# Float64 weights to float32 pairs by another chain of instructions, on ACT and DVE instead of ACT, DVE and POOL

## The chip, the core and the metric

One core of one Trainium2 chip runs the whole program. The metric is the device time of one execution in microseconds; the kernel before takes 956.41 us (median of three runs, 956.0 to 957.4). A core has five engines that run side by side, each with an in-order queue of its own: PE (matrix products, with its weight loads shown as PEld), DVE (vector), ACT (scalar), POOL (GpSimd) and SP, which here only issues DMAs. Waits between engines go by semaphores.

## The reference

```python
scores = scale * np.matmul(q, k.transpose(0, 1, 3, 2))     # 8 batches, 8 heads, 576 positions, 64 wide
mask_plain = (rel >= 0) & (rel < window)                   # window 32, heads 0 to 3
mask_dil = (rel >= 0) & (rel < window * dilation) & (rel % dilation == 0)   # dilation 4, heads 4 to 7
attn = softmax(np.where(masks, scores, -1e9))
x = np.matmul(attn, v) -> (4608, 512)
h = x @ w_in                                               # 512 to 2048
g = h * np.clip(h + 3.0, 0.0, 6.0) / 6.0
return g @ w_out                                           # 2048 to 512
```

`w_in` and `w_out` come as float64, q, k and v as float32. The kernel gets the float64 words as they are and must make float32 numbers of them on the chip.

## The kernel before, in words

**Feed-forward part.** The 4608 tokens are cut into 12 chunks of 384 (`CH`), the 2048 hidden features into 16 groups of 128 (`NF`, index f). One step is one chunk with one f: `gemm1` (lines 406 to 427) makes h of that group with 12 products of 384 columns (lines 416 to 418), then ACT adds 3 and clips at 0 (line 421, tile t), DVE clips at 6 and multiplies by h (line 422), ACT rounds to the matrix format (line 425, gh) and DVE takes the remainder (line 426, gl). `gemm2` (lines 429 to 443) adds the group's part of the output with 9 products of 512 columns (lines 437 to 439), two steps later (`LAG`). Numbers are kept as a rounded high part and a remainder, so each product is three: high by high, low by high, high by low. `gemm1` has two PSUM tiles, so the products of step n wait for line 422 of step n-2. The first two chunks run interleaved over f (lines 456 to 461), the others one after the other; there are 192 steps.

**Attention part.** The work is cut into 48 trios. The first 12 (`NFIRST`) run ahead of and into the first steps (lines 513 to 523), the rest beside the products of later steps (lines 470 to 480). A trio has scores and values on PE, turns of the tiles (line 245 on PE for the first 12), the softmax on DVE (lines 186 to 191) and ACT (line 193), the division on DVE (lines 200 to 203), and `st_split` (lines 279 to 305): ACT rounds x to xh (line 302), POOL takes the remainder xl (line 305).

**Weights.** Each f has two pieces of 128 x 512 float64 numbers, 32 pieces in all, 512 KB each. SP loads a piece into a staging tile `st` of four rows of 512 words (line 326); rows 0 and 1 hold the words as loaded, rows 2 and 3 are for work. The result goes to `wt[f]`: row 2j the rounded high part (`hi`), row 2j+1 the remainder (`lo`). Staging tiles and `wt` tiles share one pool of 18 buffers, and `wt` tiles stay, so with rising f fewer are left for staging. A conversion goes in three stages, and `convert_beat` (lines 379 to 392) advances up to three pieces by one stage each: split of one piece, join of the next, fields of the one after.

- `cv_fields` (lines 337 to 348): DVE cuts the exponent out of the high word (line 341) and the mantissa bits (line 344), ACT shifts and rebiases the exponent (line 348).
- `cv_join` (lines 350 to 359): DVE adds the low word, scaled, to the mantissa (line 352) and the sign to the exponent (line 355), POOL multiplies both (line 359).
- `cv_split` (lines 361 to 365): ACT rounds (line 363, `hi`), POOL takes the remainder (line 364, `lo`).

**Order.** Within an engine the order is set at build time from priorities: `turn_of` gives each part of a step its place, the beats come once a step and a second time in every other step until step 30 (`BEATS`, `EXTRA`), six of them ahead of the first step (`CB`). `pace` ties the first instructions of a piece, in that ordering, behind the last product that was written down before them; it adds no wait on the chip.

Of the kernel before, what the change touches and what calls it, by code (L numbers as in the profile page):

```python
# [8 lines left out]
F32 = mybir.dt.float32  # L9
F32R = mybir.dt.float32r  # L10
BF16 = mybir.dt.bfloat16
I32 = mybir.dt.int32
U32 = mybir.dt.uint32
I64 = mybir.dt.int64
AF = mybir.ActivationFunctionType
ALU = mybir.AluOpType
AX = mybir.AxisListType

P = 128
# [29 lines left out]
def windowed_attention_ffn(ctx: ExitStack, tc: tile.TileContext, qk, vp, w, mask, out):  # L49
# [23 lines left out]
    nc = tc.nc  # L73
# [20 lines left out]
    const = ctx.enter_context(tc.tile_pool(name="const", bufs=1))  # L94
# [14 lines left out]
    ident_b = mi[:, :P]  # L109
    mask_sb = mi[:, P:].rearrange("p (t x) -> p t x", t=6)  # L110
    ident = const.tile([P, P], F32, name="ident")
    rebias = const.tile([P, 1], F32, name="rebias")
    three = const.tile([P, 1], F32, name="three")


# [4 lines left out]
    for _ in range(WARM):  # L120
        nc.tensor.matmul(idle, lhsT=zeros[:, :P], rhs=zeros[:, P : P + 512], start=True, stop=True)

    nc.gpsimd.memset(rebias, -float(916 << 23))
    nc.gpsimd.memset(three, 3.0)


# [182 lines left out]
    def pace(ins):  # L309

        if "pe" in last:
            tc.add_manual_dep(
                ins.ins, last["pe"].ins.name,
                mybir.DependencyInfo(mybir.DependencyClass.NoSync, mybir.DependencyReason.DATA), reason="pace",
            )
# [5 lines left out]
    wt, staged = {}, {}  # L321
# [8 lines left out]

    def parts(p):
        st = staged[p]
        words = st[:, 0:2].rearrange("p a n -> p (a n)").bitcast(U32).rearrange("p (n w) -> p n w", w=2)
        f, j = divmod(p, 2)
        return words[:, :, 0], words[:, :, 1], st[:, 2], st[:, 3], wt[f][:, 2 * j], wt[f][:, 2 * j + 1]

    def cv_fields(p):
        if p % 2 == 0:
            wt[p // 2] = wpool.tile([P, 4, WN], F32R, name="wt", tag="w")
        _, hi_w, ex, mn, _, _ = parts(p)  # L340
        pace(nc.vector.tensor_scalar(  # L341
            out=ex.bitcast(U32), in0=hi_w, scalar1=0x7FF00000, scalar2=None, op0=ALU.bitwise_and
        ))
        pace(nc.vector.tensor_scalar(  # L344
            out=mn.bitcast(U32), in0=hi_w, scalar1=0xFFFFF, scalar2=0x100000,
            op0=ALU.bitwise_and, op1=ALU.bitwise_or,
        ))
        nc.scalar.activation(ex.bitcast(I32), ex.bitcast(I32), AF.Relu, bias=rebias, scale=8.0)

    def cv_join(p):  # L350
        lo_w, hi_w, ex, mn, _, _ = parts(p)
        nc.vector.scalar_tensor_tensor(  # L352
            out=mn, in0=lo_w, scalar=2.0**-32, in1=mn.bitcast(U32), op0=ALU.mult, op1=ALU.add
        )
        nc.vector.scalar_tensor_tensor(  # L355
            out=ex.bitcast(U32), in0=hi_w, scalar=0x80000000, in1=ex.bitcast(U32),
            op0=ALU.bitwise_and, op1=ALU.bitwise_or,
        )
        nc.gpsimd.tensor_tensor(out=mn, in0=mn, in1=ex, op=ALU.mult)  # L359

    def cv_split(p):
        _, _, _, mn, hi, lo = parts(p)
        nc.scalar.copy(hi, mn)  # L363
        nc.gpsimd.tensor_tensor(out=lo, in0=mn, in1=hi.bitcast(F32), op=ALU.subtract)  # L364
        del staged[p]


# [11 lines left out]
    def convert_beat():  # L379
        if beat["split"] < beat["join"]:  # L380
            cv_split(beat["split"])
            beat["split"] += 1
        if beat["join"] < beat["fields"]:
            cv_join(beat["join"])
            beat["join"] += 1
        p = beat["fields"]
        if p < NP:
            load_ahead(p + 1)
            if p < beat["loaded"]:
                cv_fields(p)  # L390
                beat["fields"] += 1
        load_ahead(p + (AHEAD if "g" in last else AHEAD0))
# [119 lines left out]
    n = 0  # L512
# [106 lines left out]
```

## Time and profile before

| | before |
|---|---|
| median of three runs | 956.41 us |
| the profiled execution's own time | 957.13 us |
| its span, first to last instruction | 955.3 us |
| mean granted TensorE clock | 0.983 |
| busy PE, DVE, ACT, POOL | 905.7, 486.4, 334.0, 151.7 us |
| POOL lines 359 and 364, 32 each | 44.9 and 48.4 us |
| POOL line 305, 72 in all | 59.3 us |

The page of the profile gives busy time by engine, the span in 40 slices with a digit for the busy tenths in each, and the groups of instructions by line with their count, busy time, mean time of one, and the idle time of the engine just before them. The table by windows gives the busy time of each engine in chosen stretches. Busy time of PE counts modelled ends of pipelined products, so a busy PE is not a PE at its full rate.

### The profile page before, as it was taken

The page shows a single profiled execution, that of the slowest core. Times are in us where ns is not written, and L with a number is a line of the kernel's source. Part 1 is how long each engine was busy: PE and PEld are TensorE (multiplying, and loading weights), DVE is VectorE, ACT ScalarE, POOL GpSimd, SP SyncE. Part 2 cuts the span into 40 slices and gives each one's busy share as a digit, 9 for nine tenths or more (in the row PEclk, how much of TensorE's full clock was granted, in tenths as well). Part 3 has the DMA queues.
Part 4 walks back from the last instruction along what each step waited for, and adds up shares of the span by engine and source line. Part 5 has one row for each costly group of instructions (what it writes and reads, how often), then busy time and mean ns, then how long its engine had stood idle before and what let it go on. Part 6 is the DMA issues. An engine that isn't in the chain of part 4 may idle for free.

```text
span 955.3 us, 20665 instructions
## 1 busy us (share of the span) xinstructions
PE 905.7 (95%) x8732; PEld 803.3 (84%) x8732; DVE 486.4 (51%) x934; ACT 334.0 (35%) x629; POOL 151.7 (16%) x142
## 2 busy tenths in 40 slices
PE   7687878999988999999999999999999999999998
PEld 4476767898777898899899898999989888899997
DVE  4879999823445544544543543453444444432221
ACT  3655444433223333332333333322333333322322
POOL 0667566600011000000001001000001001000000
PEclk9889999999989999999999999999999999999999
DMA  9756222102233311311311311311311310100000
GB/s 318 240 197 237 66 70 86 45 11 99 67 85 88 112 50 46 112 49 47 112 50 47 113 48 47 112 49 49 112 48 49 112 30 15 43 5 1 34 1 33
DMA packets 37676, 74.87 MB, mean 78 GB/s; under 512 B 7248, under 2 KB 16464, under 8 KB 37584
## 3 DMA queue, kind: packets, MB, share of 16 engines
q1 hardware_dynamic: 32400, 64.12, 21.4%
q10 hardware_dynamic: 5184, 9.44, 2.7%
q8 instruction: 68, 1.11, 0.5%
q14 instruction: 24, 0.20, 0.1%
HBM read 57.02 MB, written 9.44 MB: 70 GB/s over the span
## 4 chain that ended last, share of the span: by engine, by line
PE 82%; DVE 13%; issue 2%; DMA 2%; ACT 1%; SPq 0%; DVEq 0%
PE ps_o L437 13%; PE ps_h L416 13%; PE ps_h L417 13%; PE ps_h L418 13%; PE ps_o L438 12%; PE ps_o L439 12%; DVE st L344 3%; PE ps_a L174 3%; PE ps_a L156 2%; DVE st L341 2%; DVE st L355 2%; DVE st L352 2%; DVE t L422 1%; DVE gl L426 1%; DMA st<-in_w 1%
## 5 line engine op out<-in xcount | busy, mean ns | idle before, releaser
L416 PE MATMUL ps_h<-xh,wt 128*128 128x384 f32 x768 | 263.2, 343 | 21.6 <-DVE t L422 21.6
L417 PE MATMUL ps_h<-xl,wt 128*128 128x384 f32 x768 | 262.3, 342 | 0.0
L418 PE MATMUL ps_h<-xh,wt 128*128 128x384 f32 x768 | 262.1, 341 | 0.0
L422 DVE SCALAR_TENSOR_TENSOR t<-t,ps_h 128x384 f32<-128x384 f32 x192 | 105.9, 552 | 298.3 <-ACT t L421 277.8
L437 PE MATMUL ps_o<-wt,gh 128*128 128x512 f32 x576 | 229.9, 399 | 0.0
L438 PE MATMUL ps_o<-wt,gh 128*128 128x512 f32 x576 | 226.9, 394 | 0.0
L439 PE MATMUL ps_o<-wt,gl 128*128 128x512 f32 x576 | 222.1, 392 | 4.4 <-DVE gl L426 4.4
L421 ACT ACTIVATE t<-ps_h,three 128x384 f32<-128x384 f32 x192 | 111.2, 579 | 240.0 <-PE ps_h L418 237.8
L416 PEld LDWEIGHTS ps_h<-xh,wt 128*128 128x128 f32 x768 | 145.4, 189 | 34.3 <-DVE t L422 27.2
L426 DVE TENSOR_TENSOR gl<-t,gh 128x384 fp32r<-128x384 f32 x192 | 113.7, 592 | 100.4 <-ACT gh L425 100.4
L305 POOL TENSOR_TENSOR xl<-xf,xh 128x384 fp32r<-128x384 f32 (+3 forms) x72 | 59.3, 836 | 637.2 <-ACT xh L302 636.6
L425 ACT CAST gh<-t 128x384 fp32r<-128x384 f32 x192 | 98.5, 513 | 155.9 <-DVE t L422 152.9
L417 PEld LDWEIGHTS ps_h<-xl,wt 128*128 128x128 f32 x768 | 145.5, 189 | 7.1
L418 PEld LDWEIGHTS ps_h<-xh,wt 128*128 128x128 f32 x768 | 145.8, 190 | 0.2 <-POOL wt L364 0.2
L439 PEld LDWEIGHTS ps_o<-wt,gl 128*128 128x128 f32 x576 | 108.6, 189 | 28.5 <-DVE gl L426 5.7
L437 PEld LDWEIGHTS ps_o<-wt,gh 128*128 128x128 f32 x576 | 109.8, 191 | 18.3
L438 PEld LDWEIGHTS ps_o<-wt,gh 128*128 128x128 f32 x576 | 109.5, 190 | 15.9
L193 ACT ACTIVATE e<-e 128x384 f32<-128x384 f32 x48 | 25.1, 524 | 101.9 <-DVE e L189 101.9
L156 PE MATMUL ps_a<-kq 64*32 64x64 f32 x2304 | 54.7, 225 | 3.5 <-issue 3.3
L359 POOL TENSOR_TENSOR st<-st 128x512 f32<-128x512 f32 x32 | 44.9, 1405 | 43.2 <-DVE st L355 37.1
L156 PEld LDWEIGHTS ps_a<-kq 64*32 64x32 f32 x2304 | 44.5, 107 | 7.4 <-issue 6.6
L364 POOL TENSOR_TENSOR wt<-st,wt 128x512 fp32r<-128x512 f32 x32 | 48.4, 1522 | 12.3 <-ACT wt L363 12.3
(43 smaller groups left out, 544.6 us busy)
## 6 DMA issues: line engine op xcount, KB each, us to landing
kq<-in_qk SPq DMA_DIRECT2D x48, 416.0 KB, 4.6
v<-in_v SPq DMA_DIRECT2D x48, 390.0 KB, 3.6
st<-in_w SPq DMA_DIRECT2D x32, 512.0 KB, 4.6
out<-o ACTq DMA_DIRECT2D x36, 256.0 KB, 2.1
a<-a_t SPq DMA_DIRECT2D x144, 24.0 KB, 1.8
xf<-xf_t SPq DMA_DIRECT2D x144, 24.0 KB, 1.8
mi<-in_mask SPq DMA_DIRECT2D x1, 608.0 KB, 5.0
```

The lines of the kernel that those rows point to most:

```text
L156: last["pe"] = nc.tensor.matmul(ps[at : at + QB, 2 * QB * i : 2 * QB * (i + 1)], lhsT=x[rows, KW + QB * n : KW + QB * (n + 1)], rhs=x[rows ...
L305: eng.tensor_tensor(out=view(xl), in0=src, in1=view(xh).bitcast(F32), op=ALU.subtract)
L416: nc.tensor.matmul(ph, lhsT=wt[f][:, 0, ks], rhs=a, start=(kt == 0), stop=False)
L417: nc.tensor.matmul(ph, lhsT=wt[f][:, 0, ks], rhs=b, start=False, stop=False)
L418: last["pe"] = nc.tensor.matmul(ph, lhsT=wt[f][:, 1, ks], rhs=a, start=False, stop=(kt == NK - 1))
L421: nc.scalar.activation(t, ph, AF.Relu, bias=three, scale=1.0)
L422: nc.vector.scalar_tensor_tensor(out=t, in0=t, scalar=6.0, in1=ph, op0=ALU.min, op1=ALU.mult)
L425: nc.scalar.copy(gh, t)
L426: nc.vector.tensor_tensor(out=gl, in0=t, in1=gh.bitcast(F32), op=ALU.subtract)
L437: nc.tensor.matmul(po[c][tt], lhsT=gh[:, ts], rhs=wt[f][:, 2], start=(f == 0), stop=False)
L438: nc.tensor.matmul(po[c][tt], lhsT=gh[:, ts], rhs=wt[f][:, 3], start=False, stop=False)
L439: last["pe"] = nc.tensor.matmul(po[c][tt], lhsT=gl[:, ts], rhs=wt[f][:, 2], start=False, stop=(f == NF - 1))
```

## The change

The float64 number's high word, read as a float32, is multiplied by a power of two on ACT, which puts the exponent into place for a shift by three bits; the top three bits of the low word come as a rounded integer from a second ACT instruction. DVE shifts, puts the sign in, adds the integer, and takes the remainder after ACT has rounded. The two POOL instructions per piece and the constant `rebias` are gone. The loads, the beats, the tiles and everything outside these functions stay as they are.

```diff
-    rebias = const.tile([P, 1], F32, name="rebias")
...
-    nc.gpsimd.memset(rebias, -float(916 << 23))
...
     def parts(p):
         st = staged[p]
-        words = st[:, 0:2].rearrange("p a n -> p (a n)").bitcast(U32).rearrange("p (n w) -> p n w", w=2)
         f, j = divmod(p, 2)
-        return words[:, :, 0], words[:, :, 1], st[:, 2], st[:, 3], wt[f][:, 2 * j], wt[f][:, 2 * j + 1]
+        words = st[:, 0:2].rearrange("p a n -> p (a n)").rearrange("p (n w) -> p n w", w=2)
+        return words[:, :, 1], words[:, :, 0], st[:, 2], st[:, 3], wt[f][:, 2 * j], wt[f][:, 2 * j + 1]
 
     def cv_fields(p):
         if p % 2 == 0:
             wt[p // 2] = wpool.tile([P, 4, WN], F32R, name="wt", tag="w")
-        _, hi_w, ex, mn, _, _ = parts(p)
-        pace(nc.vector.tensor_scalar(
-            out=ex.bitcast(U32), in0=hi_w, scalar1=0x7FF00000, scalar2=None, op0=ALU.bitwise_and
-        ))
-        pace(nc.vector.tensor_scalar(
-            out=mn.bitcast(U32), in0=hi_w, scalar1=0xFFFFF, scalar2=0x100000,
-            op0=ALU.bitwise_and, op1=ALU.bitwise_or,
-        ))
-        nc.scalar.activation(ex.bitcast(I32), ex.bitcast(I32), AF.Relu, bias=rebias, scale=8.0)
+        hi_w, lo_w, v, a, _, _ = parts(p)
+        pace(nc.scalar.mul(v, hi_w, 2.0**-112))
+        pace(nc.scalar.mul(a.bitcast(U32), lo_w.bitcast(U32), 2.0**-29))
+        nc.vector.tensor_scalar(
+            out=v.bitcast(U32), in0=v.bitcast(U32), scalar1=3, scalar2=None, op0=ALU.logical_shift_left
+        )
 
     def cv_join(p):
-        lo_w, hi_w, ex, mn, _, _ = parts(p)
+        hi_w, _, v, a, hi, _ = parts(p)
         nc.vector.scalar_tensor_tensor(
-            out=mn, in0=lo_w, scalar=2.0**-32, in1=mn.bitcast(U32), op0=ALU.mult, op1=ALU.add
-        )
-        nc.vector.scalar_tensor_tensor(
-            out=ex.bitcast(U32), in0=hi_w, scalar=0x80000000, in1=ex.bitcast(U32),
+            out=v.bitcast(U32), in0=hi_w.bitcast(U32), scalar=0x80000000, in1=v.bitcast(U32),
             op0=ALU.bitwise_and, op1=ALU.bitwise_or,
         )
-        nc.gpsimd.tensor_tensor(out=mn, in0=mn, in1=ex, op=ALU.mult)
+        nc.vector.tensor_tensor(out=v.bitcast(U32), in0=v.bitcast(U32), in1=a.bitcast(U32), op=ALU.add)
+        nc.scalar.copy(hi, v)
 
     def cv_split(p):
-        _, _, _, mn, hi, lo = parts(p)
-        nc.scalar.copy(hi, mn)
-        nc.gpsimd.tensor_tensor(out=lo, in0=mn, in1=hi.bitcast(F32), op=ALU.subtract)
+        _, _, v, _, hi, lo = parts(p)
+        nc.vector.tensor_tensor(out=lo, in0=v, in1=hi.bitcast(F32), op=ALU.subtract)
         del staged[p]
```

## The prediction

> **What bounds the kernel now.** I read the page's slices first, then the table by windows, the groups of instructions in the stage they pointed to, the single lines with their shortest and longest times, and last the waits and the chain. The page's slices are 23.9 us each:
>
> ```profile
> span 955.3 us, 20665 instructions
> ...
> PE   7687878999988999999999999999999999999998
> PEld 4476767898777898899899898999989888899997
> DVE  4879999823445544544543543453444444432221
> ACT  3655444433223333332333333322333333322322
> POOL 0667566600011000000001001000001001000000
> ```
>
> From the ninth slice on PE is full and everything else is loosely used. In slices 3 to 7 it is DVE that stands at nine tenths, and POOL is busy in slices 2 to 8 and hardly after: this is where the weights are converted. The table by windows (busy time and count of PE, PEld, DVE, ACT, POOL, then granted clock, DMA share, GB/s) gives the stage from the end of the first step's products to the end of the conversion, and the one behind it:
>
> ```profile
> 24.00:56.50 32.50, 23.04 (x623) 18.18 (x612) 26.09 (x51) 17.30 (x34) 18.58 (x18) 0.89 0.75 246
> 56.50:191.90 135.40, 113.89 (x661) 98.55 (x662) 126.96 (x166) 65.42 (x121) 87.65 (x63) 0.95 0.31 107
> 192.00:240.00 48.00, 48.00 (x376) 43.40 (x375) 17.17 (x35) 16.09 (x30) 0.00 (x0) 1.00 0.18 62
> ```
>
> In the 135.4 us of the middle row DVE is busy for 126.96; it idles 8.4 us. Behind it PE is busy for 48.00 of 48.00. Line 422 comes once a step, so its starts give the period of a step when PE alone sets it (timeline of DVE, start and duration):
>
> ```profile
> 196.06 0.56 DVE L422 SCALAR_TENSOR_TENSOR t<-t,ps_h 128x384 f32<-128x384 f32 x1 [2.47 <-ACT t L421]
> ...
> 212.70 0.55 DVE L422 SCALAR_TENSOR_TENSOR t<-t,ps_h 128x384 f32<-128x384 f32 x1 [2.47 <-ACT t L421]
> ```
>
> Four periods lie between (starts at 196.06 and 212.70): 4.16 us a step of 21 products. Now the groups of the middle stage alone (count, busy us and mean ns):
>
> ```profile
> L364 POOL TENSOR_TENSOR wt<-st,wt 128x512 fp32r<-128x512 f32 x28 | 42.9, 1542 | 12.3 <-ACT wt L363 12.3
> L359 POOL TENSOR_TENSOR st<-st 128x512 f32<-128x512 f32 x27 | 38.2, 1414 | 33.6 <-DVE st L355 30.9 <-issue 2.1 <-DVE z L200 0.6
> L416 PE MATMUL ps_h<-xh,wt 128*128 128x384 f32 x96 | 34.6, 360 | 14.4 <-DVE t L422 14.3
> ...
> L344 DVE TENSOR_SCALAR st<-st 128x512 uint32<-128x512 uint32 x26 | 32.8, 1260 | 0.0
> L437 PE MATMUL ps_o<-wt,gh 128*128 128x512 f32 x71 | 28.9, 407 | 0.0
> ...
> L341 DVE TENSOR_SCALAR st<-st 128x512 uint32<-128x512 uint32 x26 | 23.7, 912 | 1.2 <-DMA st<-in_w 1.2
> L352 DVE SCALAR_TENSOR_TENSOR st<-st 128x512 f32<-128x512 uint32 x26 | 21.9, 842 | 0.2
> L355 DVE SCALAR_TENSOR_TENSOR st<-st 128x512 uint32<-128x512 uint32 x26 | 21.7, 835 | 0.0
> L426 DVE TENSOR_TENSOR gl<-t,gh 128x384 fp32r<-128x384 f32 x25 | 20.4, 817 | 4.7 <-ACT gh L425 4.7
> ...
> L348 ACT ACTIVATE st<-st,rebias 128x512 int32<-128x512 int32 x26 | 18.8, 723 | 28.3 <-DVE st L341 25.9 <-issue 1.6 <-ACT t L421 0.8
> L363 ACT CAST wt<-st 128x512 fp32r<-128x512 f32 x27 | 16.7, 617 | 15.5 <-POOL st L359 15.4
> ...
> L422 DVE SCALAR_TENSOR_TENSOR t<-t,ps_h 128x384 f32<-128x384 f32 x25 | 13.6, 543 | 0.9 <-ACT t L421 0.8
> ```
>
> 26 of the 32 pieces pass here. Their four DVE lines take 23.7 + 32.8 + 21.9 + 21.7 = 100.1 us, 3.85 us a piece. PE waits for line 422, which stands in DVE's queue between them. What PE itself needs: 3 x 96 products of line 416's kind and about 3 x 70 of line 437's are 499, at 21 a step 23.8 steps, at 4.16 us 99 us. The other 162 are attention's, by these pieces of the chain (start, length, count) 0.018 us each for small ones and 0.16 for a turn:
>
> ```profile
> 49.53 0.48 PE ps_a L245 x3
> 50.17 0.85 PE ps_a L156 x48
> 51.41 6.82 DMA st<-in_w
> ```
>
> At most 5.5 us, for 144 small ones and 18 turns. **PE's own floor for the stage is 104.4 us of 135.4**; 31 us is the most that can be won in it.
>
> **Why the four lines cost 3.85 us.** Shortest, median and longest of three conversion lines and of line 426:
>
> ```profile
> L344 DVE TENSOR_SCALAR st<-st x32: 414/1494/1526, 27.6 to 182.3; 128x512 uint32<-128x512 uint32 x32
> L341 DVE TENSOR_SCALAR st<-st x32: 383/773/1524, 27.2 to 180.9; 128x512 uint32<-128x512 uint32 x32
> L355 DVE SCALAR_TENSOR_TENSOR st<-st x32: 673/680/1780, 28.9 to 183.4; 128x512 uint32<-128x512 uint32 x32
> L426 DVE TENSOR_TENSOR gl<-t,gh x192: 541/559/1646, 59.0 to 946.4; 128x384 fp32r<-128x384 f32 x192
> ```
>
> The same instruction takes 0.41 or 1.5 us. The long ones lie on POOL's instructions, as here, where line 344 starts 0.18 us after line 359 and ends 0.28 us after it:
>
> ```profile
> 133.62 1.41 POOL L359 TENSOR_TENSOR st<-st 128x512 f32<-128x512 f32 x1 [0.63 <-DVE st L355]
> ...
> 133.80 1.51 DVE L344 TENSOR_SCALAR st<-st 128x512 uint32<-128x512 uint32 x1
> ```
>
> So DVE does not only carry the conversion, it also stands still while POOL works on it.
>
> **The change, part by part.** *Removed:* lines 341, 344 and 352 on DVE, 348 on ACT, 359 and 364 on POOL, and with these the cause of the long ones: in the stage POOL keeps only line 305. The memset of `rebias` goes too, at no gain, at the start, where POOL is idle. *DVE per piece after:* a shift of one contiguous operand, by lines 341 and 344 without POOL 0.38 to 0.42, I take 0.41; the sign, line 355 as it is, 0.68; an integer add and a remainder with two operands each, 0.68 by line 355 (line 426 takes 0.54 for 384 columns, so 512 is in line with that). Sum 2.45 us, 26 pieces 64 us. What DVE does besides in the stage is at least 127.0 - 100.1 = 27 us; line 426 also loses its long cases (817 against a median of 559: 25 x 0.26 = 6.5 us), which I set against the overlaps that make busy time smaller than the sum of its lines. DVE after: **91 us**, under PE's floor.
>
> *ACT per piece after:* two products in place of line 348, and the rounding, which stays but moves from split to join. Line 363 is the nearest row for a product without a bias tile: 0.617. The trace has no ACT read from SBUF with a step of two words; the nearest row of a stepped access is line 302, whose output has a step of four words (all groups of the run):
>
> ```profile
> L302 ACT CAST xh<-xf 128x288 fp32r<-128x288 f32 x16 | 11.4, 715 | 7.2 <-DMA xf<-xf_t 7.2
> ...
> L302 ACT CAST xh<-xf 128x96 fp32r<-128x96 f32 x16 | 6.0, 373 | 7.1 <-DMA xf<-xf_t 7.1
> ```
>
> (715 - 373)/192 is 1.78 ns an element, so 512 elements would take 1.11 us. Bounds 0.617 and 1.11; I take 0.62, since DVE's line 341, which reads these same words with this step, is at 0.38 no slower than line 344. ACT in the stage: 65.4 - 18.8 + 26 x 2 x 0.617 = **79 us**; at the other end 104.
>
> The Trainium skill, "SBUF — State Buffer", section Specifications, has 16-byte lines that need two hits each for full bandwidth. By it a step of two float32 words still has its two hits and the products stay at 0.62, while line 302's step has one; line 302 agrees, and no run here shows the read itself. Against the change speaks "ScalarE: Activation LUTs" in the Trainium skill, section Rules for kernel authors: products belong on VectorE. With the two at 0.41 each on DVE instead, DVE would need 91 + 21 = 112 us, over PE's floor, and the stage would be some 8 us longer; the rows of this stage, with ACT at 65 of 135 us and DVE at 127, speak for ACT.
>
> *Moved and added waits:* the shift now waits for ACT's first product, so behind it in DVE's queue stand line 422 and the softmax, and PE waits for these. The products wait for the load, where line 341 did, so lines 421 and 425 stand behind a late load on ACT. The remainder waits for ACT's rounding, with line 426 behind it. The waits of the stretch from 24 to 192 us say how late such things have been (total, times, longest):
>
> ```profile
> PE ps_h L416 <- DVE t L422: 14.3, 9, 3.3
> ...
> DVE st L341 <- DMA st<-in_w: 2.7, 2, 1.5
> ...
> PEld ps_h L418 <- POOL wt L364: 0.2, 1, 0.2
> ```
>
> The loads were late by 2.7 us in all and the finished weights by 0.2: pieces are made ahead of need, and that cover hides the longer hand-over between ACT and DVE. If it is gone, a hand-over shows with a few tenths of a microsecond each.
>
> *Sum.* Next late after DVE is PE: 104.4 us. I add the 8.4 us that even the bounding engine idled in this stage before, since three in-order queues still wait on each other: 112.8, a gain of 22.6 us; bounds 31 (no idle left) and 14 (ACT at its upper price, see below). The six pieces before 56.5 us save at most 6 x 1.4 = 8.4 us; but there the chain goes on over attention's products and a load of 6.8 us, quoted above, so I take 1.5, with 0 and 4 as bounds. From 192 us on nothing changes, since PE is full. Together 24 us: 957.1, the profiled execution's own time, becomes 933; that execution lay 0.7 us over the median of 956.4, so I forecast **932.5**. An integer add on DVE that is slower than its neighbours by x us costs 26x of DVE's slack of 13 us before it shows; the trace has none, only line 352, which takes integers into an arithmetic operation at no extra cost.
>
> **The rivals.** *ACT takes DVE's place:* at 1.11 us a product ACT needs 104 us, as much as PE, and with both full I count the idle twice: 104.4 + 16.8 = 121, a gain of 14, **943**. For it: line 302's price. Against: line 341.
>
> *Slower, through the loads:* SP can load a piece only into a free buffer, and from f = 12 on at most five are left for staging. Now a piece takes DVE so long that the load is there in time. If the faster chain empties the buffers and each of the last eight pieces finds its load just issued, ACT stands for the whole landing:
>
> ```profile
> st<-in_w SPq DMA_DIRECT2D x32, 512.0 KB, 4.6
> ```
>
> That is 8 x 4.6 = 37 us with lines 421 and 425 behind it, against 24 won: **970**. It decides from 24/26 = 0.9 us lost a piece. Against it: DVE met a late load only twice, and conversions run ahead of need, so that an order made at build time can put the products later.
>
> *Nothing gained:* PE waits for line 422 because of the loop of lines 421 and 422 over two PSUM tiles, and not because of what stands ahead of it in the queue: **956.4**. Against it: after 192 us the same loop runs without a wait, with line 422 itself idle 2.47 us a step.
>
> *A slow integer add:* at 1.41 us, what POOL takes for two operands, DVE needs 91 + 19 = 110 and the stage 118 or so: a gain of 17 + 1.5, **937**; only at 2.1 us would all be eaten up.
>
> **How the numbers follow.** Forecast 0.66, ACT bound 0.16, slow add 0.06, nothing gained 0.04, loads 0.08. Differences under 0.2% (1.9 us) can't be told from none here. Faster 0.88, same 0.04, slower 0.08. The low end is 31 + 4 us won, 922; the high end goes past the ACT case to 948, and leaves out the last two cases.
>
> **What would show it.** Right: POOL idle from about 95 us to the first later xl; shift near 0.41 and the two-operand lines near 0.68 with hardly a long case; conversion done by about 165 us with DVE near 80% busy; ACT's products at 0.62; PE's wait for line 422 under 5 us; a step of 4.2 to 4.5 us through the stage, and the part after it unchanged. Wrong: ACT products over 0.9 us, DVE or ACT idle on loads by more than 10 us, or line 422 still waited for by 14 us.

## The result

The changed kernel takes 922.99 us (median of four runs, 922.0 to 928.7) against 956.88 for the kernel before on the same chip: ratio 0.9659, 95% interval 0.9619 to 0.9699. The profiled execution took 923.19 us, with a span of 921.4 us, 33.9 less than before. The forecast was 932.5, the range 922 to 948.

The page's slices, now of 23.0 us:

```profile
span 921.4 us, 20615 instructions
...
PE   7789999999889999999999999999999999999997
PEld 4569999988778998989899888989988998899996
DVE  3778878534544544544454454445444444422221
ACT  3767666532224333234233333323333332322322
POOL 0211000000010000001000100000000010000000
```

DVE has left its row of nines: in slices 2 to 7 it stands at seven to eight tenths, and PE is full from the fourth slice on, but for the eleventh and twelfth. POOL is as good as empty after the fourth slice. The stage that the prediction took, from the first line 422 (now line 414) to the 26th, starts and ends here on DVE:

```profile
52.81 0.55 DVE L414 SCALAR_TENSOR_TENSOR t<-t,ps_h 128x384 f32<-128x384 f32 x1
...
162.57 0.56 DVE L414 SCALAR_TENSOR_TENSOR t<-t,ps_h 128x384 f32<-128x384 f32 x1 [2.44 <-ACT t L413]
```

It lasts 109.8 us instead of 135.4. The table by windows for just that stretch (busy us and count of PE, PEld, DVE, ACT, POOL, then granted clock, DMA share, GB/s):

```profile
52.81:162.57 109.76, 105.40 (x665) 95.30 (x664) 86.59 (x160) 73.17 (x141) 7.01 (x8) 0.98 0.39 134
```

PE is busy for 105.4 of 109.8, where the prediction's floor was 104.4; DVE for 86.6 instead of 127. Where PE's idle time lies shows when the stretch is cut at the second step, in the kernel before (first row) and in the changed one:

```profile
64.98:191.90 126.92, 107.92 (x572) 93.65 (x565) 119.76 (x155) 59.59 (x109) 81.42 (x58) 0.95 0.32 107
```

```profile
64.50:162.57 98.07, 97.92 (x544) 89.29 (x545) 78.05 (x144) 65.47 (x125) 5.22 (x6) 1.00 0.39 136
```

Behind the second step PE idled for 19.0 us before and idles for 0.15 us now; nearly all that is left idle lies in the 11.7 us between the first step and the second. PE's busy time in this stretch falls too, from 107.9 to 97.9 us, with the granted clock at 1.00 instead of 0.95; no run shows how much of that is the clock's.

The conversion's groups between 24 and 192 us, and line 418, which was 426:

```profile
L347 DVE SCALAR_TENSOR_TENSOR st<-st 128x512 uint32<-128x512 uint32 x32 | 22.8, 712 | 0.9
L351 DVE CUSTOM_DVE_ANT_0 st<-st 128x1024 uint16<-128x1024 uint16 x32 | 22.6, 706 | 0.8
L356 DVE TENSOR_TENSOR wt<-st,wt 128x512 fp32r<-128x512 f32 x32 | 22.6, 705 | 3.9 <-ACT wt L352 3.9
L340 ACT ACTIVATE st<-st 128x512 uint32<-128x512 uint32 x32 | 21.3, 666 | 0.0
L339 ACT ACTIVATE st<-st 128x512 f32<-128x512 f32 x32 | 21.3, 665 | 4.2 <-DMA st<-in_w 4.2
L352 ACT CAST wt<-st 128x512 fp32r<-128x512 f32 x32 | 19.9, 621 | 18.0 <-DVE st L351 17.9
...
L418 DVE TENSOR_TENSOR gl<-t,gh 128x384 fp32r<-128x384 f32 x32 | 18.0, 563 | 5.2 <-ACT gh L417 5.1
...
L341 DVE TENSOR_SCALAR st<-st 128x512 uint32<-128x512 uint32 x32 | 13.6, 424 | 6.7 <-ACT st L339 6.5
```

The 32 pieces cost DVE 2.55 us each (0.424 + 0.712 + 0.706 + 0.705) instead of 3.69 over the same window before (3.85 in the stage alone), and line 418 is back at 0.563 from 0.817. The integer add of 32-bit words shows as one instruction over twice as many 16-bit words, at the price of its neighbours. The two products on ACT take 0.665 us against 0.621 for line 352, which reads without a step. The waits between 24 and 192 us, one row of the kernel before ahead of those of the changed one (us in total, times, longest):

```profile
PEld ps_h L416 <- DVE t L422: 18.7, 11, 3.7
```

```profile
ACT t L413 <- PE ps_h L410: 30.5, 22, 2.4
DVE t L414 <- ACT t L413: 24.5, 19, 2.4
...
DVE st L341 <- ACT st L339: 6.5, 4, 3.1
...
ACT st L339 <- DMA st<-in_w: 4.2, 3, 3.1
...
PEld ps_h L408 <- DVE t L414: 0.4, 1, 0.4
```

The direction has turned: line 414 waits for ACT and ACT waits for PE's products. PE's weight loads wait for line 414 for 0.4 us where it was 18.7, and the products themselves, which waited 14.3 us for it, no longer stand in the list. The wait for loads has moved from DVE (2.7 us before) to ACT (4.2 us). One of these waits stands in the chain, which here is given with start, length and work:

```profile
49.44 6.28 DMA st<-in_w
55.74 0.66 ACT st L339
56.43 0.44 DVE st L341
```

Step by step against the kernel before: the first line 414 comes 3.7 us sooner (52.81 against 56.51), the stage is 25.6 us shorter, and the other 4.6 of the 33.9 us come after it, although PE was full there before. Of the 3.7 us only 0.5 are left at the second step (64.50 against 64.98), with the wait for that load in between. The 4.6 us do not come at one place: from the 33rd step to the last the lead grows from 29.6 to 34.2 us at an even rate.

### The profile page after: what moved, and what is told of

The parts are those of the page before. It is cut to its first block, busy times and chain, and to the rows that moved or that the text cites. A ratio compares the mean times of both kernels' runs of the same rounds, so it can differ in the third digit from the quotient of the medians.

```text
span 921.4 us, 20615 instructions
## 1 busy us (share of the span) xinstructions
PE 892.1 (97%) x8732; PEld 795.2 (86%) x8732; DVE 447.5 (49%) x934; ACT 348.1 (38%) x661; POOL 58.9 (6%) x77
## 4 chain that ended last, share of the span: by engine, by line
PE 93%; DVE 3%; DMA 2%; ACT 1%; issue 0%; SPq 0%; DVEq 0%
PE ps_o L429 15%; PE ps_h L408 15%; PE ps_h L409 14%; PE ps_h L410 14%; PE ps_o L430 14%; PE ps_o L431 14%; PE ps_a L172 3%; PE ps_a L154 2%; DMA st<-in_w 1%; DMA kq<-in_qk 1%; PE ps_a L243 1%; DVE x L201 1%; PE ps_a L164 1%; DVE st L347 1%; DMA mi<-in_mask 1%
## 5 line engine op out<-in xcount | busy, mean ns | idle before, releaser
L418 DVE TENSOR_TENSOR gl<-t,gh 128x384 fp32r<-128x384 f32 x192 | 107.3, 559 | 95.2 <-ACT gh L417 95.1
L300 ACT CAST xh<-xf 128x384 fp32r<-128x384 f32 (+3 forms) x72 | 33.6, 533 | 48.9 <-DMA xf<-xf_t 48.7
L172 PEld LDWEIGHTS ps_a<-v,a 64*32 64x32 f32 x1728 | 36.1, 105 | 10.7 <-issue 10.7
```

What stands on the lines that cost most here:

```text
L172: last["pe"] = nc.tensor.matmul(ps[at : at + QB, i * W : (i + 1) * W], lhsT=ats[t][rows, QB * n : QB * (n + 1)], rhs=vs[t][rows, n, :], st ...
L418: nc.vector.tensor_tensor(out=gl, in0=t, in1=gh.bitcast(F32), op=ALU.subtract)
```

## The experiments

All ratios are to the kernel before, on the chip of that run; the runs are spread over several chips, so kernels from different sections are compared by their ratios. The main theory after the first comparison was: in the stage PE's own rate decides as soon as DVE's work is under it, and what DVE lost before was standstill behind POOL. The rivals were that fewer instructions or the hand-overs between engines count by themselves. The growth of the lead behind the stage had a theory of its own: chance of the run or the chip.

### Both kernels again, on one chip

> The kernel before, unchanged, beside the changed kernel on one chip. It is here for the part of the gain that lies behind the conversion: 4.6 us of the 33.9 us between the two profiled spans came as a steady 0.03 us a step from step 32 to step 191 (17.97 against 17.85 us for four steps). Theory: this belongs to the run or the chip, not to the change, so on one chip four late steps take the same within 0.03 us in both kernels. Rival: the change does something to every later step, and the 0.12 us per four steps shows again. Span near 955.

> The changed kernel, unchanged. Theory: the gain is 25.6 us in the stage of conversion, 3.7 us ahead of it and about nothing behind it, some 29 us against the kernel before on the same chip, ratio near 0.970. Rival: late steps are shorter by the change, ratio 0.965 again on any chip.

Measured: 956.56 us for the kernel before (one run), 923.74 for the changed one, ratio 0.9648 (0.9630 to 0.9666). The 61st and the 181st step on DVE, first in the kernel before, then in the changed one:

```profile
362.74 0.55 DVE L422 SCALAR_TENSOR_TENSOR t<-t,ps_h 128x384 f32<-128x384 f32 x1 [2.40 <-ACT t L421]
...
898.91 0.56 DVE L422 SCALAR_TENSOR_TENSOR t<-t,ps_h 128x384 f32<-128x384 f32 x1 [2.47 <-ACT t L421]
```

```profile
332.05 0.55 DVE L414 SCALAR_TENSOR_TENSOR t<-t,ps_h 128x384 f32<-128x384 f32 x1 [2.36 <-ACT t L413]
...
864.54 0.55 DVE L414 SCALAR_TENSOR_TENSOR t<-t,ps_h 128x384 f32<-128x384 f32 x1 [2.43 <-ACT t L413]
```

120 steps (the work of attention among them) take 536.17 against 532.49 us, as in the first two profiles (536.18 and 532.76). My theory fell: the 0.03 us a step belongs to the kernel. On PE the first of twelve products of a step and the first product behind them start here:

```profile
549.45 0.34 PE L416 MATMUL ps_h<-xh,wt 128*128 128x384 f32 x1
...
551.57 0.39 PE L437 MATMUL ps_o<-wt,gh 128*128 128x512 f32 x1
```

```profile
513.39 0.34 PE L408 MATMUL ps_h<-xh,wt 128*128 128x384 f32 x1
...
515.48 0.39 PE L429 MATMUL ps_o<-wt,gh 128*128 128x512 f32 x1
```

2.12 against 2.09 us for twelve: 2.5 ns a product. The nine products of the second kind take 2.04 us in both.

### Where the tiles lie

The change takes away one constant, `rebias`, of one word in each partition. The allocation gives it 32 bytes, so every tile behind it (weights, staging, work, loads) moves down by 32 bytes; `xh` and `xl` stay. That the tiles stay as they are, as was said of the change, does therefore not hold for their addresses. Two kernels move only that. On PE, DVE, ACT and SP the instructions stand in the same order as in the kernel that each is made from, and POOL has at most a memset at the start more.

```diff
--- the changed kernel
+    rebias = const.tile([P, 1], F32, name="rebias")
...
+    nc.gpsimd.memset(rebias, -float(916 << 23))
--- the kernel before
-    rebias = const.tile([P, 1], F32, name="rebias")
...
+    behind = ctx.enter_context(tc.tile_pool(name="behind", bufs=1))    # the last pool in SBUF
+    rebias = behind.tile([P, 1], F32, name="rebias")
```

> The changed kernel with the unused constant rebias kept, and nothing else: the order of the instructions on every engine is the same, but every tile behind the constants (weights, work, loads) lies 32 bytes further on in each partition, where it lay before the change. In the first four profiles, four late steps took 17.97 us in both kernels of the old chain and 17.85 in both of the new one. Theory of places: the late rate follows where the tiles lie, so steps 60 to 180 take 536.2 us as before instead of 532.5, and the time is 4 to 6 us over the changed kernel: 927 to 930. Rival (the numbers in the weight tiles, made by another arithmetic, or the order of the queues set the rate): steps 60 to 180 stay at 532.5, the time at 923.

> The kernel before with rebias moved behind all other tiles, and nothing else: same order on every engine, all other tiles 32 bytes lower, where the changed kernel has them. Theory of places: steps 60 to 180 take 532.5 us instead of 536.2, and the time is 4 to 6 us under the kernel before: 951 to 953. Rival (numbers or queues): no change, 956 to 957.

Measured: 930.37 us (ratio 0.9710, 0.9678 to 0.9743) for the changed kernel with the old places, 952.90 us (0.9945, 0.9927 to 0.9963) for the kernel before with the new ones. The same two steps, in the one and in the other:

```profile
334.83 0.55 DVE L414 SCALAR_TENSOR_TENSOR t<-t,ps_h 128x384 f32<-128x384 f32 x1 [2.40 <-ACT t L413]
...
871.00 0.55 DVE L414 SCALAR_TENSOR_TENSOR t<-t,ps_h 128x384 f32<-128x384 f32 x1 [2.47 <-ACT t L413]
```

```profile
363.22 0.56 DVE L422 SCALAR_TENSOR_TENSOR t<-t,ps_h 128x384 f32<-128x384 f32 x1 [2.36 <-ACT t L421]
...
895.71 0.56 DVE L422 SCALAR_TENSOR_TENSOR t<-t,ps_h 128x384 f32<-128x384 f32 x1 [2.44 <-ACT t L421]
```

536.17 and 532.49 us: the late rate follows the places to the hundredth, in both directions, and neither the chain nor the numbers. The other profiles agree: these 120 steps take 536.17 to 536.48 us in the four profiles with the old places and 532.48 to 532.85 us in the ten with the new ones. So 32 bytes are worth 4.5 us on the kernel before, and about 6 on the changed one (ratios 0.9710 and 0.9648, from two chips, the first with a wide interval). Where between stationary operand, moving operand and address the 2.5 ns arise was not tried.

### POOL out of the old chain

```diff
-        nc.gpsimd.tensor_tensor(out=mn, in0=mn, in1=ex, op=ALU.mult)
+        nc.vector.tensor_tensor(out=mn, in0=mn, in1=ex, op=ALU.mult)
...
-        nc.gpsimd.tensor_tensor(out=lo, in0=mn, in1=hi.bitcast(F32), op=ALU.subtract)
+        nc.vector.tensor_tensor(out=lo, in0=mn, in1=hi.bitcast(F32), op=ALU.subtract)
```

> The old chain with its two POOL instructions moved to DVE: POOL no longer stands in DVE's way, but DVE has six instructions a piece. Theory (the sum of DVE's own time decides): 0.41 + 0.42 + 4 x 0.68 = 3.55 us a piece against 3.85 with the standstills, so the stage is shorter by 26 x 0.3 = 8 us and line 426 gives 4 to 6 more: 943 to 948 us. Rival (the standstills behind POOL are the whole matter, and the new arithmetic is worth nothing by itself): 923 to 930. Second rival (the hand-overs to POOL cost nothing, and six instructions on DVE are worse than four): no faster than 955.

Measured: 930.75 us, ratio 0.9721 (0.9705 to 0.9737): 0.75 us above the first rival's range and 12 below the theory's. The old four lines, between 24 and 192 us (count, busy us, mean ns), first in the kernel before and then in this one:

```profile
L344 DVE TENSOR_SCALAR st<-st 128x512 uint32<-128x512 uint32 x32 | 37.6, 1177 | 0.0
...
L341 DVE TENSOR_SCALAR st<-st 128x512 uint32<-128x512 uint32 x32 | 27.5, 858 | 2.7 <-DMA st<-in_w 2.7
...
L355 DVE SCALAR_TENSOR_TENSOR st<-st 128x512 uint32<-128x512 uint32 x32 | 26.8, 838 | 0.0
L352 DVE SCALAR_TENSOR_TENSOR st<-st 128x512 f32<-128x512 uint32 x32 | 26.0, 813 | 0.3
```

```profile
L352 DVE SCALAR_TENSOR_TENSOR st<-st 128x512 f32<-128x512 uint32 x32 | 22.7, 708 | 0.1
...
L355 DVE SCALAR_TENSOR_TENSOR st<-st 128x512 uint32<-128x512 uint32 x32 | 22.3, 696 | 0.0
...
L344 DVE TENSOR_SCALAR st<-st 128x512 uint32<-128x512 uint32 x32 | 15.3, 477 | 0.0
L341 DVE TENSOR_SCALAR st<-st 128x512 uint32<-128x512 uint32 x32 | 14.8, 461 | 1.1 <-DMA st<-in_w 1.1
```

The same four instructions cost 2.34 us a piece (0.708 + 0.696 + 0.477 + 0.461) that cost 3.69 over all 32 pieces before (0.813 + 0.838 + 1.177 + 0.858): 32 x 1.35 = 43 us were standstill behind POOL. And in the stage:

```profile
57.91:167.75 109.84, 106.44 (x672) 96.23 (x673) 106.47 (x209) 63.13 (x117) 7.99 (x8) 1.00 0.37 124
```

109.8 us, as in the changed kernel, with DVE at 106.5 instead of 86.6. My sum had 127 for it. It added durations, while these instructions overlap at their ends (0.68 us long, but 0.60 us from start to start), it took 26 pieces where 25 fall into the stage, and it added 8.4 us of idle time: behind the second step PE is busy here for 99.86 of 99.86 us, and DVE for 97.2. This kernel still has the old places of the tiles. Its partner is the changed kernel with the old places: 930.75 against 930.37 us on another chip, ratios 0.9705 to 0.9737 and 0.9678 to 0.9743. **With the tiles in the same places, the times show no worth of the new arithmetic beyond taking POOL out; they could hide some 4 us.** The profiles hint at such an amount: the 26th step comes at 165.1 us in that partner and at 167.8 here.

### One POOL instruction back

```diff
-        nc.vector.tensor_tensor(out=lo, in0=v, in1=hi.bitcast(F32), op=ALU.subtract)
+        nc.gpsimd.tensor_tensor(out=lo, in0=v, in1=hi.bitcast(F32), op=ALU.subtract)
```

> The changed kernel with the remainder of the weights on POOL instead of DVE. Theory: DVE is relieved of 0.68 us a piece and stands still for about 0.84 us a piece behind POOL (half of 3.85 less 2.18, for one POOL instruction of two), so DVE's sum changes by +4 us in the stage, stays under PE's floor, and the time stays within 3 us of the changed kernel: 921 to 927. Rival (any POOL instruction in the chain is dear, for the lock and for its 1.5 us of hand-over): 930 or more.

Measured: 923.81 us, ratio 0.9643 (0.9629 to 0.9658), as the theory has it. The standstills are back, in the add (shortest, median, longest) as in the stage's sum:

```profile
L351 DVE CUSTOM_DVE_ANT_0 st<-st x32: 677/690/1593, 32.7 to 171.7; 128x1024 uint16<-128x1024 uint16 x32
```

```profile
54.98:166.36 111.38, 107.60 (x671) 97.05 (x671) 93.72 (x140) 75.52 (x145) 42.69 (x34) 0.97 0.39 134
```

The add takes up to 1.59 us again and DVE has 93.7 us of work and standstill, but that is under PE's 104, and the time is that of the changed kernel on the same chip (923.74). So one POOL instruction in the chain is not dear as such; the 127 us that two of them made of DVE's time were.

### The two products on DVE

```diff
-        pace(nc.scalar.mul(v, hi_w, 2.0**-112))
-        pace(nc.scalar.mul(a.bitcast(U32), lo_w.bitcast(U32), 2.0**-29))
+        pace(nc.vector.tensor_scalar(out=v, in0=hi_w, scalar1=2.0**-112, scalar2=None, op0=ALU.mult))
+        pace(nc.vector.tensor_scalar(out=a.bitcast(U32), in0=lo_w.bitcast(U32), scalar1=2.0**-29, scalar2=None, op0=ALU.mult))
```

> The changed kernel with the two products of each piece on DVE instead of ACT. Theory (what counts is whether DVE's own work stays under PE's floor in the stage): DVE has 86.6 us of work in the stage of 109.8 us, and 25 pieces x 2 x 0.35 from start to start add 18, so DVE comes to 104, about PE's floor; the stage lengthens by 0 to 5 us and the time is 923 to 929. If the old sum (idle time on top of the larger of two) decided, the stage would be 8 us longer and the time 931 or more. Rival (a product is better on VectorE, since two hand-overs from ACT go): 919 to 922.

Measured: 926.67 us, ratio 0.9665 (0.9642 to 0.9688), inside the theory's range and not told apart from the changed kernel (0.9630 to 0.9666).

```profile
56.18:167.06 110.88, 106.52 (x671) 96.06 (x670) 97.88 (x208) 47.97 (x92) 6.57 (x8) 0.98 0.39 131
```

DVE at 97.9 us is still under PE, and the stage is 110.9. A product takes 0.46 us on DVE against 0.67 on ACT. The rule that products belong on VectorE (the Trainium skill, "ScalarE: Activation LUTs", section Rules for kernel authors) gives no gain in the kernel's time here, and the 8 us that I had as its price do not show either.

### Three more instructions on DVE

```diff
+        nc.vector.tensor_tensor(out=a, in0=v, in1=hi.bitcast(F32), op=ALU.subtract)    # three times, in cv_split
```

> The changed kernel with three more DVE instructions a piece (the remainder taken again, into a tile that nobody reads). Theory (DVE's work is free up to PE's floor, and costs in full beyond it): about 24 pieces x 3 x 0.61 = 44 us on top of 86.6 in the stage of 109.8, so 131 us of DVE against 105 of PE: the stage grows by 21 to 25 us and the early part by up to 9, to 947 to 958 us. Rival (every instruction of the conversion costs its time): 32 x 1.83 = 58 us, 980 or more. Second rival (DVE has more room than its busy time says): under 935.

Measured: 949.49 us, ratio 0.9912 (0.9897 to 0.9928).

```profile
63.67:187.43 123.76, 113.07 (x681) 97.42 (x682) 123.00 (x230) 73.26 (x142) 7.57 (x8) 0.99 0.31 109
```

Here DVE is the bound again, busy for 123.0 of 123.8 us, with 14 us more stage than the changed kernel, 11 us more ahead of it (the line that was 414 first comes at 63.7) and 2 more behind it. The time is in the theory's range, but not by its split, which had 21 to 25 us in the stage and at most 9 ahead of it. 32 x 3 x 0.61 = 59 us of work cost some 26: in the stage, what lay under PE's floor was free; ahead of the first step, where DVE's work stands in the chain, there is no such floor.

### No conversion

```diff
-        pace(nc.scalar.mul(v, hi_w, 2.0**-112))
-        pace(nc.scalar.mul(a.bitcast(U32), lo_w.bitcast(U32), 2.0**-29))
...
+        pace(nc.scalar.copy(hi, hi_w))
+        pace(nc.scalar.copy(lo, hi_w))
```

> The changed kernel with the conversion left out: ACT copies the high words into both halves of the weight tile, twice 0.67 us a piece, and DVE has nothing to do for the weights. The loads, the beats and all products stay; the weights are not the reference's. It shows how much the conversion still costs. Theory (PE's floor is reached): the stage from the first to the 26th line 414 falls from 109.7 to no less than 104, and the attention ahead of the first step, in whose chain DVE's four instructions of some pieces stand, ends 3 to 8 us sooner: 911 to 918. Rival (the hand-overs of the conversion still hold PE up in the stage): under 908. Second rival (the loads and not the conversion set the early part): 920 to 923.

Measured: 918.07 us, ratio 0.9582 (0.9565 to 0.9599), 0.07 us above the theory's range.

```profile
54.14:159.36 105.22, 104.61 (x661) 95.15 (x662) 32.98 (x62) 61.39 (x118) 6.21 (x8) 0.98 0.37 130
```

The stage is 105.2 us with PE busy for 104.6: this is the floor, and the changed kernel stands 4.5 us above it. All of that lies between the first two steps, for behind the second the stretch is as long as the changed kernel's 98.07 us:

```profile
61.34:159.36 98.02, 98.02 (x556) 89.25 (x546) 29.56 (x54) 56.90 (x108) 4.82 (x6) 1.00 0.39 135
```

So from the second step to the 26th the conversion costs nothing any more. The early part does not end sooner (first line at 54.1): ACT waits there for 9.0 us at one load, with its line for the first step behind it in the queue.

### Loads earlier

```diff
-LD = (2, 3, 4, 6, 14)
+LD = (2, 3, 4, 6, 7, 9)            # two loads earlier
+LD = (2, 3, 4, 6, 8, 8, 10, 10)    # four loads earlier
...
-CB = (6, 7, 8, 8, 10, 11)
+CB = (8, 9, 9, 10, 11, 11)         # conversion later, with two loads earlier
```

> The changed kernel with LD = (2, 3, 4, 6, 7, 9) instead of (2, 3, 4, 6, 14): two loads of weight pieces stand further forward in SP's queue, ahead of loads of attention that wait for a buffer. In the changed kernel ACT's first product waits 3.1 us for a load issued at 49.4 us and landed at 55.7, with line 417 behind it. Theory: this wait goes, the second step, which comes 11.7 us after the first, comes 3 us sooner, and the time falls to 919 to 922. Rival (the DMA engines are full in the early part, so that one load sooner is another later): 922 to 926.

> As the run with two loads earlier, and CB = (8, 9, 9, 10, 11, 11) instead of (6, 7, 8, 8, 10, 11): the first six beats of the conversion stand later in the attention ahead of the first step. Without any conversion the early attention ran 6 us ahead at 40 us and then waited for loads. Theory: of the conversion in that chain 2 to 4 us go, 916 to 920, as far as the loads are there. Rival (the first step then waits for its weights): 923 or more.

> The changed kernel with LD = (2, 3, 4, 6, 8, 8, 10, 10): four loads further forward, in pairs. Theory: as with two loads, 919 to 922. Rival (a pair ahead of attention's loads delays these by the 2 us that each piece takes at 250 GB/s, and the early attention with them): 923 to 927.

Measured: 921.38 (ratio 0.9627, 0.9608 to 0.9646), 921.64 (0.9625, 0.9608 to 0.9642) and 925.53 us (0.9671, 0.9651 to 0.9690). With two loads earlier ACT's wait for loads between 24 and 75 us is down from 3.7 to 0.6 us, and the stage is at the floor:

```profile
ACT st L339 <- DMA st<-in_w: 0.6, 1, 0.6
```

```profile
57.24:162.65 105.41, 103.36 (x661) 93.79 (x662) 85.70 (x158) 72.92 (x140) 7.07 (x8) 1.00 0.37 127
```

But the first line 414 comes at 57.2 instead of 52.8, the second at 64.6 (64.5 in the changed kernel) and the 26th at 162.7 (162.6): the shorter stage is only a later start. The first kernel's time is in the theory's range, but its second step does not come 3 us sooner, as the theory had it. The second kernel fell between its theory (916 to 920) and its rival (923 or more). These two have the lowest medians of all that do the whole work, but their intervals overlap with the changed kernel's; whether they beat it is left open. Four loads earlier gain nothing, as the rival had it.

## Why the prediction was right, and where its sizes were off

The mechanism held: DVE bounded the stage, a good part of its time was standstill behind POOL, the change takes both down, and PE's own rate takes over at 104 us. The sign and the range held; the forecast gain of 24 us was measured as 33.9, close to the range's low end, and 4.6 us of it come from a part that the prediction had put at nothing. By its steps:

- **DVE's sum after, 91 us:** 86.6 measured. The shift at 0.424 (0.41), the three others at 0.705 to 0.712 (0.68); the sum is smaller all the same because durations overlap and because 24 pieces pass in the shorter stage and not 26. The slow integer add did not come.
- **ACT's sum, 79 us:** 73.2, with products at 0.665, near the lower of the two bounds, and 24 or 25 pieces. ACT never came near PE's 104 us, so that rival fell; the row of the same words read by DVE was the better neighbour than line 302.
- **"104.4 + 8.4 us of idle":** 109.8 measured, so the idle time to be added was 5.4 us and the stage's gain 25.6, not 22.6. The addition was no sound step: behind the second step PE, which now bounds, idles for 0.15 us, and for nothing in the kernel without POOL in the old chain. What is left lies between the first two steps, where ACT waits 3.1 us for a load. Idle time of the engine that bounded before was no toll that the next one paid.
- **The early part, 1.5 us (0 to 4):** 3.7 measured at the first step, inside the bounds, but 0.5 at the second.
- **"From 192 us on nothing changes, since PE is full":** this step failed. A full PE got 0.7% faster there, because the removed constant had held all later tiles 32 bytes further on; 4.6 us of the 33.9. The memset of `rebias` was booked at no gain; its tile was not looked at.
- **The loads rival, 970 us:** its mechanism is there, in small: ACT waits 4.2 us for loads, 3.1 of them once with line 417 queued behind, but nearly all in the first steps and none from f = 12 on.
- **"Nothing gained":** refuted by PE's wait for line 414, which is down to 0.4 us.
- **Conversion done by 165 us:** it ended at 175. No product waits for a weight tile in the list of waits, so this cost nothing.
- **Readings and sums:** DVE's nines stand in slices 4 to 7; slice 3 has a seven. By the prediction's own terms the slow add comes to 938 us and not 937, and the ACT rival's 943 leaves out the 1.5 us of the early part. None of this moves the forecast.

What the prediction could not know from its rows is the split that the experiments give: of some 34 us about 27 come from taking POOL out of DVE's way (957.48 to 930.75 with the old arithmetic and old places), some 4.5 to 6 from the places of the tiles, and from the smaller number of DVE instructions nothing that the times can tell from zero, at most some 4.

## What to carry to other kernels

Take each engine's busy time over the stage, with overlaps counted once, and go by the largest. In every kernel here without the old pair of POOL instructions, the stretch from the second step to the 26th was as long as the largest, within 0.5 us, and work on an engine under it was free. This did not hold with the pair: the kernel before needed 126.9 us with DVE busy for 119.8. The arithmetic of this chain mattered less than which engine it made stand still. Before a faster sequence of instructions is credited, move the old one off the shared engine and time that; and when a change adds or drops a tile, however small, compare the rate in a part of the run that the change does not touch.

## What the runs showed of the hardware that was not expected

- **Places of tiles.** With the same order of instructions on PE, 32 bytes of shift of all tiles behind the constants changed twelve of a step's 21 products by 2.5 ns each (2.12 against 2.09 us for twelve) and left the other nine at 2.04 us; 0.5% of the kernel's time, in both directions. The rate of the late steps goes by the places in all fourteen profiles. Why is open.
- **DVE behind POOL.** The same one-operand instruction takes 0.41 us alone and 1.5 beside a POOL instruction; two-operand ones go from 0.68 up to 1.78, the add in the run with one POOL instruction from 0.69 to 1.59. The Trainium skill, "SBUF — State Buffer", section SBUF: two separate sides, has the two engines share a pair of ports that one holds for a whole instruction while the other stands; these times agree. Over the 32 pieces it came to 43 us of DVE's time.
- **Integer add.** A 32-bit integer add of 512 words ran as 1024 16-bit words in 0.706 us, no more than the float32 subtraction's 0.705.
